# A new SBUF layout for the weight squares and the moved rows of an attention and MLP-mixer kernel

## The chip, the cores and the metric

The kernel runs on one core of a Trainium2 chip. The metric is device time in microseconds (us) of one execution. Engines are named as in the profile: PE is TensorE (PEld its weight loads), DVE VectorE, ACT ScalarE, POOL GpSimd, and SP the engine whose queue issues the loads. SBUF is the on-chip memory that the engines read from, PSUM the accumulators that TensorE writes.

## What is computed

Linear attention over 8 batches, 8 heads, 576 positions and 64 dimensions a head; its result goes through a token mixer and a channel mixer. All inputs are float32 (the weights arrive as 64-bit floats and are made narrower on the chip). Cut to what matters:

```
q_s = softmax(q, over dims);  k_s = softmax(k, over positions)
x   = q_s @ (k_s.T @ v)                          # [8, 576, 512]
u   = x + (relu(x.T @ w_tok1) @ w_tok2).T        # token mixer, 576 -> 256 -> 576
out = u + relu(u @ w_ch1) @ w_ch2                # channel mixer, 512 -> 1536 -> 512
```

## The kernel before

Products that need float32's precision are made of three: each factor is split into a high part (rounded to the type fp32r) and a low part (the rest), and high x high, low x high and high x low are summed in PSUM. `split` (L105, L106) does this: ScalarE copies the high part, VectorE subtracts it from the source and writes the low part.

**Units.** A unit is one batch and one pair of heads; there are 32. Each runs softmax of k and q, then four stages on TensorE: s1 (turning q, and k x v, L268), s2 (L328, the first token product), s3 (L336, and the first half of L373), s4 (the second half of L373). The first 8 units (two batches) are done in plain float32 while the weights arrive; the other 24, the late ones, are put between the steps described next by a table of places (`put`). A late unit's q is turned by VectorE and ScalarE (L306, L314) and split into `qth` and `qtl`. Stage L373 leaves `u`, turned and split, in the tiles `uh` and `ul`: four rows of 512 columns a group of 512 positions, three pairs of such tiles in turn.

**Steps.** The channel mixer runs over 9 groups of 512 positions and, for each, over 12 slices `f` of 128 hidden channels: 108 steps. A step is `ch1` and, one step behind, `ch2`.

- `ch1` (L402) makes 12 matmuls into one bank of PSUM: for each of four `n`, `c1h` x `uh`, `c1l` x `uh`, `c1h` x `ul`. What is held in TensorE is a square of weights (128 x 128, 512 bytes in each partition); what is moved through it is a row of `uh` or `ul` (512 columns, 2 KiB in each partition). ScalarE (L405) and VectorE (L406) then write relu of the result, split, to `h2h` and `h2l` (2 KiB each).
- `ch2` (L415) makes 12 matmuls into four banks, three for each `n`: `c2h` x `h2h`, `c2l` x `h2h`, `c2h` x `h2l`.

While a matmul moves its row, the next matmul's square is loaded; in the trace each weight load begins within 0.01 us of the start of the matmul ahead of it. So at each time TensorE reads two places of SBUF: the row of this matmul and the square of the next one.

**Weights.** `load_ch(f)` loads, narrows and splits the two slices of a step: 512 columns each of `w_ch1` and `w_ch2`. Slices 0 to 3 are loaded while the last early units run, 4 to 11 ahead of steps 1, 2, 4, 5, 7, 8, 10 and 11. Steps 0 to 3 are group 0, slices 0 to 3; then group 1 runs all slices, then group 0 the other eight, then the groups 2 to 8.

**Order and places.** The order of each engine's instructions is chosen when the program is built, by a scheduler that keeps the dependencies. The pools decide the addresses. In the built program the places in a partition are, modulo 2 KiB: squares n of `c1h` and `c1l` at 1536 + 512n; squares n of `c2h` and `c2l` at 1920 + 512n; the rows of `uh`, `ul`, `h2h`, `h2l` all at 1920. By **distance** the prediction means the start of the moved row less the start of the square loaded meanwhile, modulo 2 KiB. While square n of `ch1` is loaded it is 1920 - 1536 - 512n, so 384, 1920, 1408 and 896 for n = 0 to 3; in `ch2` it is -512n, so 0, 1536, 1024 and 512. Where a `ch1` matmul loads a square of `ch2` it is 0, and where a `ch2` matmul loads a square of `ch1` 384.

Of the kernel before, what the change touches and what calls it, by code (L numbers as in the profile page):

```python
# [8 lines left out]
F32 = mybir.dt.float32  # L9
F32R = mybir.dt.float32r  # L10
# [5 lines left out]
P = 128  # L16
CW = 512
# [3 lines left out]
def attn_mixer_kernel(ctx: ExitStack, tc: tile.TileContext, q, k, kt, v, wt, out, dims):  # L21
# [3 lines left out]
    nc = tc.nc  # L25
    B, H, S, D, TOK, DM, DCH, wide = dims
    NJ = DM // P
    NF = DCH // P
# [8 lines left out]
    F_HEAD, F_MORE = 4, 8  # L37

    const = ctx.enter_context(tc.tile_pool(name="const", bufs=1))
# [3 lines left out]
    sm = ctx.enter_context(tc.tile_pool(name="sm", bufs=2))  # L43
    stg = ctx.enter_context(tc.tile_pool(name="stg", bufs=2))
    cv = ctx.enter_context(tc.tile_pool(name="cv", bufs=2))
    upool = ctx.enter_context(tc.tile_pool(name="upool", bufs=1))
    hpool = ctx.enter_context(tc.tile_pool(name="hpool", bufs=2))
    ps_o = ctx.enter_context(tc.tile_pool(name="ps_o", bufs=NJ, space=bass.MemoryType.PSUM))
    ps_h = ctx.enter_context(tc.tile_pool(name="ps_h", bufs=4, space=bass.MemoryType.PSUM))

# [19 lines left out]
    def kv_tile(pool, i):  # L70

        t = pool.tile([P, P], F32, name=f"kvf{i}")
        nc.gpsimd.memset(t, 0.0)
        return t

    kv_ring = [kv_tile(const, 0)]

    w1h = const.tile([P, C, TOK], F32R, name="w1h")
    w1l = const.tile([P, C, TOK], F32R, name="w1l")
    w1th = const.tile([P, TOK], F32R, name="w1th")  # L80
    w1tl = const.tile([P, TOK], F32R, name="w1tl")
    w2h = const.tile([P, NT, S], F32R, name="w2h")
    w2l = const.tile([P, NT, S], F32R, name="w2l")
    c1h = const.tile([P, NF, NJ, P], F32R, name="c1h")
    c1l = const.tile([P, NF, NJ, P], F32R, name="c1l")
    c2 = {}

    def c2_rows(f0, f1):
        late = ctx.enter_context(tc.tile_pool(name=f"late{f0}", bufs=1))
        h_ = late.tile([P, f1 - f0, DM], F32R, name=f"c2h{f0}")  # L90
        l_ = late.tile([P, f1 - f0, DM], F32R, name=f"c2l{f0}")
        for f in range(f0, f1):
            c2[f] = h_[:, f - f0, :], l_[:, f - f0, :]

    c2_rows(0, F_HEAD)
    part = const.tile([P, NJ, CW], F32, name="part")

    Q = 32

    def f32(ap):  # L100
        return ap.bitcast(F32)

    def split(hi, lo, src, lo_eng):

        nc.scalar.copy(hi, src)  # L105
        lo_eng.tensor_tensor(lo, src, f32(hi), op=ALU.subtract)  # L106
# [3 lines left out]
    def ps_unit(dtype=F32):  # L110

        pools = unit_banks[0]
        pool, name = pools[turn[0] % len(pools)]
        turn[0] += 1
        return pool.tile([P, 512], dtype, name=name)
# [33 lines left out]
    def load_weights(i, n=CW, out=None):  # L149

        if not wide:
            t = out if out is not None else cv.tile([P, C1 * P], F32, name="cv_s")[:, 0:n]
            nc.sync.dma_start(t, wt[i][:, 0:n])
            return t
        conv.append(conv.pop(0))
        raw = conv[-1][0].tile([P, CW, 2], U32, name="stg")
        nc.sync.dma_start(raw[:, 0:n, :].rearrange("p n w -> p (n w)"), wt[i][:, 0:n].bitcast(U32))
        return narrow(raw, n, out)

    def narrow(raw, n, out):  # L160


        w0, w1 = raw[:, 0:n, 0], raw[:, 0:n, 1]
        s = conv[-1][1].tile([P, C1 * P], U32, name="cv_s")[:, 0:n]
        nc.vector.tensor_scalar(s, w1, 20, 0x7FF, op0=ALU.logical_shift_right, op1=ALU.bitwise_and)
        nc.scalar.activation(s, s, AF.Relu, bias=ebias, scale=2.0**23)
        nc.vector.scalar_tensor_tensor(s, w1, 0x80000000, s, op0=ALU.bitwise_and, op1=ALU.bitwise_or)
        nc.vector.tensor_scalar(w1, w1, 0xFFFFF, 0x100000, op0=ALU.bitwise_and, op1=ALU.bitwise_or)
        f1 = w1.bitcast(F32)
        nc.vector.scalar_tensor_tensor(f1, w0, 2.0**-32, w1, op0=ALU.mult, op1=ALU.add)  # L170
        z = s.bitcast(F32) if out is None else out
        nc.vector.tensor_tensor(z, f1, s.bitcast(F32), op=ALU.mult)
        return z
# [3 lines left out]
    AT_T1, AT_T2, AT_TAIL, AT_C1 = 0, N1, N1 + NT, N1 + NT + 2  # L177
    AT_C2 = AT_C1 + NF
# [18 lines left out]
        split(w2h[:, :, S0:S], w2l[:, :, S0:S], t, nc.vector)  # L197

    def load_ch(f):
        h_, l_ = (w[:, f].rearrange("p n m -> p (n m)") for w in (c1h, c1l))  # L200
        split(h_, l_, load_weights(AT_C1 + f), nc.vector)
        split(*c2[f], load_weights(AT_C2 + f), nc.vector)


    def softmax_k(u):
        ktt = u["kt"]
        mc = sm.tile([P, 1], F32, name="mc")
        nc.vector.tensor_reduce(mc, ktt, axis=AX.X, op=ALU.max)
        kx = u["k"]
        if u["early"]:  # L210
            nc.vector.tensor_scalar(mc, mc, -1.0, None, op0=ALU.mult)
            nc.scalar.activation(ktt, ktt, AF.Exp, bias=mc)
            t = ps_unit()
            for c in range(C):
                nc.tensor.transpose(t[:, c * P : (c + 1) * P], ktt[:, c * P : (c + 1) * P], f32(ident))
            nc.scalar.copy(kx[:, 0:C, :], t.rearrange("p (c d) -> p c d", c=C))
            t = ps_unit()
            nc.tensor.transpose(t[:, 0:P], ktt[:, S0 : S0 + P], f32(ident))
            nc.scalar.copy(kx[:, C, :], t[:, 0:P])
            return  # L220

        dg = sm.tile([P, P], F32, name="dg", bufs=1)
        nc.scalar.activation(dg, f32(ident), AF.Copy, scale=mc)
        t = ps_unit()
        nc.tensor.matmul(t[:, 0:P], ones, dg, start=True, stop=True)  # L225
        mb = sm.tile([P, P], F32, name="mb", bufs=1)
        nc.scalar.copy(mb, t[:, 0:P])  # L227
        nc.gpsimd.tensor_tensor(kx, kx, mb.unsqueeze(1).broadcast_to([P, C1, P]), op=ALU.subtract)  # L228
        nc.scalar.activation(kx, kx, AF.Exp)
# [115 lines left out]
        u["hh"], u["hl"] = hh, hl  # L345


    slots = [tuple(upool.tile([P, NJ, CW], F32R, name=f"u{x}{i}") for x in "hl") for i in range(3)]
    uT = [slots[i] for i in (0, 1, 2, 1, 0, 2, 1, 0, 2)]
    assert len(uT) == NG  # L350

# [40 lines left out]
            yield  # L392

    def ch1(g, f):
        hh = hpool.tile([P, CW], F32R, name="h2h")
        hl = hpool.tile([P, CW], F32R, name="h2l")
        t = ps_h.tile([P, 512], F32, name="ps_h")
        i = 0
        for n in range(NJ):
            uh, ul = (x[:, n, :] for x in uT[g])  # L400
            for a, w in ((c1h, uh), (c1l, uh), (c1h, ul)):
                nc.tensor.matmul(t, a[:, f, n, :], w, start=(i == 0), stop=(i == 3 * NJ - 1))  # L402
                i += 1
        drained[:] = [
            nc.scalar.activation(hh, t, AF.Relu).ins,  # L405
            nc.vector.scalar_tensor_tensor(hl, t, 0.0, f32(hh), op0=ALU.max, op1=ALU.subtract).ins,  # L406
        ]
        return hh, hl

    def ch2(acc, f, first, last, hh, hl):  # L410

        for n, o in enumerate(acc):
            cs = slice(n * P, (n + 1) * P)
            for i, (a, w) in enumerate(((c2[f][0], hh), (c2[f][1], hh), (c2[f][0], hl))):
                nc.tensor.matmul(o, a[:, cs], w, start=(first and i == 0), stop=(last and i == 2))  # L415

    def stage_rows():

# [97 lines left out]
                split_tok1()  # L516
    early_pools.close()
    del v_ring[1:], kv_ring[1:]
    ld = ctx.enter_context(tc.tile_pool(name="ld", bufs=2))
    wk = ctx.enter_context(tc.tile_pool(name="wk", bufs=1))  # L520
    c2_rows(F_HEAD, F_MORE)
    more_pools = ExitStack()
    stg_more = more_pools.enter_context(tc.tile_pool(name="stg_more", bufs=2))
    cv_more = more_pools.enter_context(tc.tile_pool(name="cv_more", bufs=2))
# [4 lines left out]
    steps = [(0, f) for f in range(F_HEAD)] + [(1, f) for f in range(NF)] + [(0, f) for f in range(F_HEAD, NF)]  # L529
# [14 lines left out]
    for n in range(NE, NU):  # L544
        b, j = divmod(n, NJ)
        if b == 2:
            at = (n0 - 10, n0 - 9, n0 - 9, n0 - 7.5) if j == 0 else [n0 - 9.5 + 2 * j + x for x in (0, 0.5, 1, 1.5)]
        else:
            at = [n0 + (b - 3) * NF + 3 * j + x for x in (0, 1, 1.5, 2)]
# [10 lines left out]
    for i, (g, f) in enumerate(steps):  # L560
        if i in load_at:
            if load_at[i] == F_MORE:
                more_pools.close()
                conv[:] = [(stg, cv)]
                c2_rows(F_MORE, NF)
            with behind(drained):
                load_ch(load_at[i])
        h = ch1(g, f)
        for fn in todo.pop(i, []):
            fn()  # L570
        if pend is not None:
            ch2(*pend[1:])
            if pend[0] != g:
                out_end(*pend[:2], i != F_HEAD)
        for fn in todo.pop(i + 0.5, []):
            fn()
        last = i + 1 == len(steps) or steps[i + 1][0] != g
        if pend is None or pend[0] != g:
            acc = [ps_o.tile([P, CW], F32, name="ps_o") for _ in range(NJ)]
        pend = (g, acc, f, pend is None or pend[0] != g, last, *h)  # L580
        if last and g > 1:
            residual(g)
# [60 lines left out]
```

## Time and profile before

| | us |
|---|---|
| executions | 834.90, 835.94, 837.50 |
| their median | 835.94 |
| the profiled execution: its span, first instruction to last | 835.7 |
| TensorE busy in the span | 805.4 |
| VectorE busy | 490.0 |
| ScalarE busy | 330.6 |

The page has one time for the profiled execution, its span. The slices of the page cut the span into 40 equal parts of 20.9 us; a digit is the busy share in tenths. The first two slices are the start (loads, first softmax); up to some 200 us the weights are converted on VectorE while the early units and the first steps run; behind that the steps and the late units alternate; the last 140 us are steps alone.

### The profile page before, as it was taken

The page shows a single profiled execution, that of the slowest core. Times are in us where ns is not written, and L with a number is a line of the kernel's source. Part 1 is how long each engine was busy: PE and PEld are TensorE (multiplying, and loading weights), DVE is VectorE, ACT ScalarE, POOL GpSimd, SP SyncE. Part 2 cuts the span into 40 slices and gives each one's busy share as a digit, 9 for nine tenths or more (in the row PEclk, how much of TensorE's full clock was granted, in tenths as well). Part 3 has the DMA queues.
Part 4 walks back from the last instruction along what each step waited for, and adds up shares of the span by engine and source line. Part 5 has one row for each costly group of instructions (what it writes and reads, how often), then busy time and mean ns, then how long its engine had stood idle before and what let it go on. Part 6 is the DMA issues. An engine that isn't in the chain of part 4 may idle for free.

```text
span 835.7 us, 11793 instructions
## 1 busy us (share of the span) xinstructions
PE 805.4 (96%) x4464; PEld 671.2 (80%) x4464; DVE 490.0 (59%) x1084; ACT 330.6 (40%) x822; POOL 113.2 (14%) x93
## 2 busy tenths in 40 slices
PE   3799999989999999999999999999999999999997
PEld 2588888777888888788888888888888888888885
DVE  6899998999775555655556554755565323012112
ACT  6876443554543344334434343444434421101110
POOL 1000000113220111311112111311131102001000
PEclk9999999999999999999999999999999999999999
DMA  8653523424212122322232211322131001001001
GB/s 269 204 144 111 201 103 99 130 62 137 85 41 94 56 62 54 105 62 62 62 112 62 62 51 33 106 61 61 32 96 46 15 1 51 1 0 51 1 1 50
DMA packets 60632, 63.54 MB, mean 76 GB/s; under 512 B 40864, under 2 KB 40992, under 8 KB 60576
## 3 DMA queue, kind: packets, MB, share of 16 engines
q1 hardware_dynamic: 55392, 53.36, 21.8%
q10 hardware_dynamic: 5184, 9.44, 3.0%
q8 instruction: 35, 0.57, 0.3%
q14 instruction: 21, 0.17, 0.1%
HBM read 53.35 MB, written 9.44 MB: 75 GB/s over the span
## 4 chain that ended last, share of the span: by engine, by line
PE 81%; DVE 8%; DMA 5%; ACT 3%; issue 2%; POOL 1%; SPq 1%; DVEq 0%; POOLq 0%; ACTq 0%
PE ps_h L402 32%; PE ps_o L415 31%; PE ps_h L373 6%; PE ps_h L328 5%; DVE q_t L314 2%; DMA q_t<-in_q 2%; PE ps_h L268 2%; DMA out<-stg 2%; PE ps_h L336 1%; ACT q_t L242 1%; PE ps_o L373 1%; PE ps_h L225 1%; DMA kt_t<-in_kt 1%; DVE st L236 1%; DVE qtl L106 1%
## 5 line engine op out<-in xcount | busy, mean ns | idle before, releaser
L406 DVE SCALAR_TENSOR_TENSOR h2l<-ps_h,h2h 128x512 fp32r<-128x512 f32 x108 | 74.3, 688 | 176.5 <-ACT h2h L405 176.5
L402 PE MATMUL ps_h<-uh,c1h 128*128 128x512 f32 x432 | 171.8, 398 | 0.0
L402 PE MATMUL ps_h<-ul,c1h 128*128 128x512 f32 x432 | 171.4, 397 | 0.0
L402 PE MATMUL ps_h<-uh,c1l 128*128 128x512 f32 x432 | 171.3, 396 | 0.0
L415 PE MATMUL ps_o<-h2h,c2h 128*128 128x512 f32 x432 | 169.2, 394 | 1.0 <-ACT h2h L405 1.0
L405 ACT ACTIVATE h2h<-ps_h 128x512 fp32r<-128x512 f32 x108 | 64.4, 597 | 266.0 <-PE ps_h L402 255.4
L415 PE MATMUL ps_o<-h2h,c2l 128*128 128x512 f32 x432 | 168.5, 391 | 0.0
L415 PE MATMUL ps_o<-h2l,c2h 128*128 128x512 f32 x432 | 152.1, 396 | 0.0
L314 DVE COPY q_t<-cv_s 32x160 f32<-32x160 f32 (+1 forms) x264 | 70.4, 267 | 61.7 <-POOL ql L106 58.4
L402 PEld LDWEIGHTS ps_h<-ul,c1h 128*128 128x128 f32 x432 | 81.8, 189 | 19.4
L415 PEld LDWEIGHTS ps_o<-h2h,c2h 128*128 128x128 f32 x432 | 81.2, 188 | 18.4 <-ACT h2h L405 1.4
L402 PEld LDWEIGHTS ps_h<-uh,c1l 128*128 128x128 f32 x432 | 81.9, 189 | 16.9
L402 PEld LDWEIGHTS ps_h<-uh,c1h 128*128 128x128 f32 x432 | 81.6, 189 | 17.1
L415 PEld LDWEIGHTS ps_o<-h2h,c2l 128*128 128x128 f32 x432 | 81.2, 188 | 16.8
L415 PEld LDWEIGHTS ps_o<-h2l,c2h 128*128 128x128 f32 x432 | 79.6, 188 | 16.4
L228 POOL TENSOR_TENSOR k_t<-k_t,mb 128x640 f32<-128x640 f32 x24 | 38.3, 1595 | 318.6 <-ACT mb L227 304.8
L106 POOL TENSOR_TENSOR ql<-q_t,qh 128x640 fp32r<-128x640 f32 x24 | 37.6, 1568 | 196.9 <-ACT qh L105 164.3
L428 POOL TENSOR_TENSOR stg<-uh,ul 128x512 f32<-128x512 f32 x28 | 35.5, 1289 | 144.6 <-DMA out<-stg 81.5
L236 DVE TENSOR_REDUCE st<-q_t 128x10 f32<-128x640 f32 x32 | 26.2, 818 | 40.3 <-DMA q_t<-in_q 40.3
L314 ACT COPY q_t<-cv_s 32x128 f32<-32x128 f32 (+1 forms) x120 | 36.8, 307 | 2.3 <-DVE cv_s L306 0.9
L247 ACT ACTIVATE q_t<-q_t 128x640 f32<-128x640 f32 x28 | 20.7, 740 | 42.9 <-DVE q_t L246 42.9
L373 PE MATMUL ps_h<-w2l,hh 128*128 128x256 f32 (+1 forms) x112 | 32.7, 296 | 0.1
(146 smaller groups left out, 1163.0 us busy)
## 6 DMA issues: line engine op xcount, KB each, us to landing
stg<-in_w SPq DMA_DIRECT2D x28, 512.0 KB, 3.4
kt_t<-in_kt SPq DMA_DIRECT2D x32, 320.0 KB, 3.4
q_t<-in_q SPq DMA_DIRECT2D x32, 320.0 KB, 2.9
v_t<-in_v SPq DMA_DIRECT2D x64, 128.0 KB, 3.0
out<-stg ACTq DMA_DIRECT2D x32, 256.0 KB, 2.8
k_t<-in_k SPq DMA_DIRECT2D x24, 320.0 KB, 3.6
v_t<-in_v SPq DMA_DIRECT2D x32, 32.0 KB, 3.1
out<-part ACTq DMA_DIRECT2D x4, 256.0 KB, 2.9
```

The lines of the kernel that those rows point to most:

```text
L106: lo_eng.tensor_tensor(lo, src, f32(hi), op=ALU.subtract)
L228: nc.gpsimd.tensor_tensor(kx, kx, mb.unsqueeze(1).broadcast_to([P, C1, P]), op=ALU.subtract)
L236: nc.vector.tensor_reduce(st[:, 0, :], qt, axis=AX.X, op=ALU.max)
L247: nc.scalar.activation(qc, qc, AF.Exp)
L314: eng(qx[ys, 0:n, xs], turned[xs, 0:n, ys])
L328: nc.tensor.matmul(y[:, 0:TOK], a, w, start=(i == 0), stop=(i == len(mm) - 1))
L373: nc.tensor.matmul(t[:, 0:N], a, w, start=(i == 0), stop=(i == len(mm) - 1))
L402: nc.tensor.matmul(t, a[:, f, n, :], w, start=(i == 0), stop=(i == 3 * NJ - 1))
L405: nc.scalar.activation(hh, t, AF.Relu).ins,
L406: nc.vector.scalar_tensor_tensor(hl, t, 0.0, f32(hh), op0=ALU.max, op1=ALU.subtract).ins,
L415: nc.tensor.matmul(o, a[:, cs], w, start=(first and i == 0), stop=(last and i == 2))
L428: nc.gpsimd.tensor_tensor(res[n], f32(uh), f32(ul), op=ALU.add)
```

## The change

The change lays the same data elsewhere and swaps the order of two matmuls. The number of instructions on each engine stays what it was (4002 matmuls and branches, 1086 rows on VectorE, 820 on ScalarE, 216 on SP, 98 on GpSimd).

1. The four squares of a step and an n stand side by side in one tile, 2 KiB: `c1h`, `c1l`, `c2h`, `c2l` at 0, 512, 1024, 1536 behind its start (`ch_rows`, index x = 0 to 3). Both slices of the weights go with the pools `late0`, `late4` and `late8`; before, `c1h` and `c1l` had places of their own for all slices.
2. `uh`, `ul`, `h2h` and `h2l` come from one pool with small tiles between them (`dg`, `mb`, `kvf0`) that shift the starts. `h2` is a pair of tiles in turn.
3. The low square comes first: in `ch1` `c1l` x `uh`, `c1h` x `uh`, `c1h` x `ul`; in `ch2` likewise.
4. The pool of the slices 4 to 7 is opened ahead of the pools of the late units, not behind them.

```diff
+    slots = [[None, None] for _ in range(3)]
+    for i in range(3):
+        slots[i][0] = lay.tile([P, NJ, CW], F32R, name=f"uh{i}")
+    dg = lay.tile([P, P], F32, name="dg")
+    for i in range(3):
+        slots[i][1] = lay.tile([P, NJ, CW], F32R, name=f"ul{i}")
+    mb = lay.tile([P, P], F32, name="mb")
+    h2 = [[lay.tile([P, CW], F32R, name=f"h2h{i}"), None] for i in range(2)]
+    kv_ring = [kv_tile(lay, 0)]
+    for i in range(2):
+        h2[i][1] = lay.tile([P, CW], F32R, name=f"h2l{i}")
...
-        h_ = late.tile([P, f1 - f0, DM], F32R, name=f"c2h{f0}")
-        l_ = late.tile([P, f1 - f0, DM], F32R, name=f"c2l{f0}")
+        t = late.tile([P, f1 - f0, NJ, 4, P], F32R, name=f"cw{f0}")
         for f in range(f0, f1):
-            c2[f] = h_[:, f - f0, :], l_[:, f - f0, :]
+            cw[f] = [t[:, f - f0, :, x, :] for x in range(4)]
...
     def load_ch(f):
-        h_, l_ = (w[:, f].rearrange("p n m -> p (n m)") for w in (c1h, c1l))
-        split(h_, l_, load_weights(AT_C1 + f), nc.vector)
-        split(*c2[f], load_weights(AT_C2 + f), nc.vector)
+        for x, at in ((0, AT_C1), (2, AT_C2)):
+            t = load_weights(at + f).rearrange("p (n m) -> p n m", n=NJ)
+            split(cw[f][x], cw[f][x + 1], t, nc.vector)
...
-            for a, w in ((c1h, uh), (c1l, uh), (c1h, ul)):
-                nc.tensor.matmul(t, a[:, f, n, :], w, start=(i == 0), stop=(i == 3 * NJ - 1))
+            for x, w in ((1, uh), (0, uh), (0, ul)):
+                nc.tensor.matmul(t, cw[f][x][:, n, :], w, start=(i == 0), stop=(i == 3 * NJ - 1))
...
-            for i, (a, w) in enumerate(((c2[f][0], hh), (c2[f][1], hh), (c2[f][0], hl))):
-                nc.tensor.matmul(o, a[:, cs], w, start=(first and i == 0), stop=(last and i == 2))
+            for i, (x, w) in enumerate(((3, hh), (2, hh), (2, hl))):
+                nc.tensor.matmul(o, cw[f][x][:, n, :], w, start=(first and i == 0), stop=(last and i == 2))
...
+    ch_rows(F_HEAD, F_MORE)
     ld = ctx.enter_context(tc.tile_pool(name="ld", bufs=2))
     wk = ctx.enter_context(tc.tile_pool(name="wk", bufs=1))
-    c2_rows(F_HEAD, F_MORE)
```

In the built program the places are now, modulo 2 KiB: squares `c1h`, `c1l`, `c2h`, `c2l` of every n at 1920, 384, 896 and 1408; rows of `uh` at 384, of `ul` at 896, of `h2h` at 1408, of `h2l` at 1920. So the distance is 512 for every n while a matmul of `ch1` loads the next square of `ch1`, and while one of `ch2` loads the next of `ch2`; it is 1536 where the one passes into the other. `w1h`, `w1l`, `w2h` and `w2l` stand 512 bytes lower than before, and the late units' tiles where they stood.

What the scheduler made of it shows in two places. First TensorE's order at the end of the last `ch1` of the program and the start of the `ch2` behind it, before (names with `_` and a number are tiles):

```order
L402 MATMUL ps_h<-uh_116,c1l 128x512
L402 MATMUL ps_h<-ul_117,c1h 128x512
L402 MATMUL ps_h<-uh_116,c1h 128x512
L402 MATMUL ps_h<-uh_116,c1l 128x512
L402 MATMUL ps_h<-ul_117,c1h 128x512
L415 MATMUL ps_o<-h2h,c2h_1377 128x512
L415 MATMUL ps_o<-h2h,c2l_1378 128x512
L415 MATMUL ps_o<-h2l,c2h_1377 128x512
```

and with the change, where one tile `cw` holds all four squares (so the two matmuls on `uh`, low square then high, read alike and stand as one row x2):

```order
L407 MATMUL ps_h<-uh_102,cw_1362 128x512 x2
L407 MATMUL ps_h<-ul_106,cw_1362 128x512
L407 MATMUL ps_h<-uh_102,cw_1362 128x512 x2
L407 MATMUL ps_h<-ul_106,cw_1362 128x512
L419 MATMUL ps_o<-h2h_108,cw_1362 128x512 x2
L419 MATMUL ps_o<-h2l_112,cw_1362 128x512
```

The sequence of rows moved (`uh`, `uh`, `ul`; `h2h`, `h2h`, `h2l`) is the same; only the squares ahead of it have changed places. Behind some 220 us of the profile before, every engine's order is the same as before but for this.

The second place is the first late unit. Before, TensorE reaches its first use of `qth` so:

```order
L328 MATMUL ps_h<-w1tl,qh 128x256
L415 MATMUL ps_o<-h2l,c2h_1377 128x512 x4
L402 MATMUL ps_h<-uh_114,c1l 128x512
L402 MATMUL ps_h<-ul_115,c1h 128x512
...
L336 MATMUL ps_h<-kvf_96,ys 128x128 x2
L373 MATMUL ps_h<-qth,kvh 128x320
L402 MATMUL ps_h<-uh_112,c1h 128x512
```

and with the change so (L335 was L328, L343 was L336, L379 was L373, L407 was L402):

```order
L335 MATMUL ps_h<-w1th,qh 128x256
L335 MATMUL ps_h<-w1tl,qh 128x256
L343 MATMUL ps_h<-kvf_110,ys 128x128 x2
L379 MATMUL ps_h<-qth,kvh 128x320
L407 MATMUL ps_h<-uh_100,cw_1067 128x512 x2
```

The four `ch2` and eleven `ch1` matmuls that stood between the unit's stages s2 and s3 now stand ahead of s2; the number of matmuls ahead of `qth` is 729 in both. VectorE there, before (c2l is the last split of weights):

```order
L306 STREAM_TRANSPOSE cv_s<-q_t 128x640
L106 TENSOR_TENSOR c2l_1378<-cv_s,c2h_1377 128x512
L106 TENSOR_TENSOR qtl<-q_t,qth 128x576
L314 COPY q_t<-cv_s 32x5x32 x6
L406 SCALAR_TENSOR_TENSOR h2l<-ps_h,h2h 128x512
```

and with the change:

```order
L313 STREAM_TRANSPOSE cv_s<-q_t 128x640
L115 TENSOR_TENSOR qtl<-q_t,qth 128x576
L115 TENSOR_TENSOR cw_1362<-cv_s,cw_1362 128x4x128
L351 SCALAR_TENSOR_TENSOR hl<-ps_h,hh 128x256
L321 COPY q_t<-cv_s 32x5x32 x6
```

The unit's low half `qtl` has passed the last split.

More of the change, by code (lines that the diff above doesn't have):

```diff
@@ L45, in attn_mixer_kernel @@
     cv = ctx.enter_context(tc.tile_pool(name="cv", bufs=2))
-    upool = ctx.enter_context(tc.tile_pool(name="upool", bufs=1))
-    hpool = ctx.enter_context(tc.tile_pool(name="hpool", bufs=2))
+    lay = ctx.enter_context(tc.tile_pool(name="lay", bufs=1))
     ps_o = ctx.enter_context(tc.tile_pool(name="ps_o", bufs=NJ, space=bass.MemoryType.PSUM))
@@ L74, in kv_tile @@
         return t
-    kv_ring = [kv_tile(const, 0)]
     w1h = const.tile([P, C, TOK], F32R, name="w1h")
@@ L83, in attn_mixer_kernel, with ch_rows @@
     w2l = const.tile([P, NT, S], F32R, name="w2l")
[L84 to L88, printed above, removed]
+    part = const.tile([P, NJ, CW], F32, name="part")
+    slots = [[None, None] for _ in range(3)]
[9 more added lines that the diff above has]
+        h2[i][1] = lay.tile([P, CW], F32R, name=f"h2l{i}")
+    cw = {}
+    def ch_rows(f0, f1):
         late = ctx.enter_context(tc.tile_pool(name=f"late{f0}", bufs=1))
-        h_ = late.tile([P, f1 - f0, DM], F32R, name=f"c2h{f0}")
-        l_ = late.tile([P, f1 - f0, DM], F32R, name=f"c2l{f0}")
+        t = late.tile([P, f1 - f0, NJ, 4, P], F32R, name=f"cw{f0}")
         for f in range(f0, f1):
-            c2[f] = h_[:, f - f0, :], l_[:, f - f0, :]
-    c2_rows(0, F_HEAD)
-    part = const.tile([P, NJ, CW], F32, name="part")
+            cw[f] = [t[:, f - f0, :, x, :] for x in range(4)]
+    ch_rows(0, F_HEAD)
     Q = 32
@@ L220, in softmax_k @@
             return
-        dg = sm.tile([P, P], F32, name="dg", bufs=1)
         nc.scalar.activation(dg, f32(ident), AF.Copy, scale=mc)
@@ L225, in softmax_k @@
         nc.tensor.matmul(t[:, 0:P], ones, dg, start=True, stop=True)
-        mb = sm.tile([P, P], F32, name="mb", bufs=1)
         nc.scalar.copy(mb, t[:, 0:P])
@@ L345, in stage_h1 @@
         u["hh"], u["hl"] = hh, hl
-    slots = [tuple(upool.tile([P, NJ, CW], F32R, name=f"u{x}{i}") for x in "hl") for i in range(3)]
     uT = [slots[i] for i in (0, 1, 2, 1, 0, 2, 1, 0, 2)]
@@ L394, in ch1 @@
     def ch1(g, f):
-        hh = hpool.tile([P, CW], F32R, name="h2h")
-        hl = hpool.tile([P, CW], F32R, name="h2l")
+        hh, hl = h2[steps.index((g, f)) % 2]
         t = ps_h.tile([P, 512], F32, name="ps_h")
@@ L412, in ch2 @@
         for n, o in enumerate(acc):
-            cs = slice(n * P, (n + 1) * P)
-            for i, (a, w) in enumerate(((c2[f][0], hh), (c2[f][1], hh), (c2[f][0], hl))):
-                nc.tensor.matmul(o, a[:, cs], w, start=(first and i == 0), stop=(last and i == 2))
+            for i, (x, w) in enumerate(((3, hh), (2, hh), (2, hl))):
+                nc.tensor.matmul(o, cw[f][x][:, n, :], w, start=(first and i == 0), stop=(last and i == 2))
     def stage_rows():
@@ L564, in attn_mixer_kernel @@
                 conv[:] = [(stg, cv)]
-                c2_rows(F_MORE, NF)
+                ch_rows(F_MORE, NF)
             with behind(drained):
```

## The prediction

> **What bounds the kernel now.** I read the page's engine table first, then the slices, then the chain that ended last, and last the groups of instructions.
>
> ```profile
> PE 805.4 (96%) x4464; PEld 671.2 (80%) x4464; DVE 490.0 (59%) x1084; ACT 330.6 (40%) x822; POOL 113.2 (14%) x93
> PE   3799999989999999999999999999999999999997
> DVE  6899998999775555655556554755565323012112
> PEclk9999999999999999999999999999999999999999
> PE 81%; DVE 8%; DMA 5%; ACT 3%; issue 2%; POOL 1%; SPq 1%; DVEq 0%; POOLq 0%; ACTq 0%
> L402 PE MATMUL ps_h<-uh,c1h 128*128 128x512 f32 x432 | 171.8, 398 | 0.0
> L415 PE MATMUL ps_o<-h2h,c2l 128*128 128x512 f32 x432 | 168.5, 391 | 0.0
> ```
>
> TensorE is busy 96% of the span at the full granted clock, makes 81% of the chain, and the groups of L402 and L415, six of 432 matmuls each (2592 in all), wait for nobody. A duration (398 ns) overlaps the next matmul, so it says nothing of the pace. The pace is in the chain in order of time, where consecutive matmuls of one line stand as one piece (start, length, what):
>
> ```profile
> 109.88 7.44 PE ps_h L402 x32
> 117.33 5.45 PE ps_o L415 x24
> ...
> 254.39 5.47 PE ps_o L415 x24
> ...
> 761.29 2.80 PE ps_h L402 x12
> 764.09 2.76 PE ps_o L415 x12
> ...
> 775.15 2.73 PE ps_o L415 x12
> 777.88 2.80 PE ps_h L402 x12
> 780.68 2.76 PE ps_o L415 x12
> ```
>
> This is what I argue from. Shape, type and clock are the same in every piece, nobody waits, yet L402 runs at 2.80/12 = 233.3 ns a matmul (7.44/32 = 232.5) and L415 at 2.76/12 = 230.0, at 2.73/12 = 227.5 in one step, and at 5.45/24 = 227.1 and 5.47/24 = 227.9 where 24 of them follow each other. Near the end, where almost only TensorE works, 2.80 and 2.76 alternate, so it is no disturbance by other engines. Something in the two lines' operands costs L402 some 6 ns each time, and L415 some 3 ns after a change from the other line, and it dies out as the run of L415 gets longer. One matmul at a time (timeline, TensorE's rows; start, length):
>
> ```profile
> 752.81 0.40 PE L415 MATMUL ps_o<-h2h,c2h 128*128 128x512 f32 x1
> 753.05 0.39 PE L415 MATMUL ps_o<-h2h,c2l 128*128 128x512 f32 x1
> 753.27 0.39 PE L415 MATMUL ps_o<-h2l,c2h 128*128 128x512 f32 x1
> ...
> 754.66 0.39 PE L415 MATMUL ps_o<-h2l,c2h 128*128 128x512 f32 x1
> 754.89 0.39 PE L415 MATMUL ps_o<-h2h,c2h 128*128 128x512 f32 x1
> 755.11 0.39 PE L415 MATMUL ps_o<-h2h,c2l 128*128 128x512 f32 x1
> 755.34 0.40 PE L415 MATMUL ps_o<-h2l,c2h 128*128 128x512 f32 x1
> 755.57 0.40 PE L402 MATMUL ps_h<-uh,c1h 128*128 128x512 f32 x1
> 755.81 0.40 PE L402 MATMUL ps_h<-uh,c1l 128*128 128x512 f32 x1
> ```
>
> From start to start the group begins with 0.24 and 0.22, ends with 0.23, 0.22 and 0.23 (754.66 to 755.34: 0.68/3 = 227), and the first of L402 takes 0.24. What differs between the lines is the place of the moved row against the square loaded meanwhile: in L415 the distance is always a multiple of 512 bytes (0, 1536, 1024, 512 modulo 2 KiB as n goes from 0 to 3), in L402 at the last of its twelve alone (else 384, 1920, 1408, 896: 384 modulo 512). So I read: at multiples of 512 the pace settles at 227 ns within some eight matmuls, whichever multiple it is; at 384 modulo 512 it never settles and averages 233.
>
> **The change part by part.** *The layout, L402.* All distances of L402 become 512 modulo 2 KiB, at the step's last matmul 1536: multiples of 512. By the reading above its matmuls go from 232.5 to 233.3 down to 227.1, and 1296 x 5.4 to 6.2 ns = 7.0 to 8.1 us are gone. I take 7.6.
>
> *The layout, L415.* It is no longer thrown off by L402 before it. Its groups stand at 230.0 where L402 comes first and at 227.9 where 24 run on; the gain is 1296 x 0.8 to 2.9 = 1.0 to 3.8 us. I take 2.4, the middle, since both kinds recur all along. Both lines together: 10.0 us.
>
> *What is not realized.* Until about 212 us VectorE sets the pace, and a faster TensorE only waits longer:
>
> ```profile
> 160.00:212.00 52.00, 48.21 (x287) 40.02 (x286) 47.50 (x101) 26.18 (x64) 10.95 (x7) 0.97 0.34 105
> 0.00:200.00 200.00, 58.12 (x226) 43.43 (x227) 0.99 0.48 149
> 200.00:836.00 636.00, 266.38 (x1072) 198.78 (x1070) 1.00 0.18 53
> PE ps_h L373 <- ACT qth L105: 2.6, 1, 2.6
> ```
>
> The first row is the table by stretches (length, then busy us of TensorE, weight loads, VectorE, ScalarE, GpSimd): VectorE works 47.5 of 52 us, converting the last weights and turning the first late head pair. The next two are the same table for L402 alone: 226 of 1298 records, 17%, lie before 200 us. I take 17% of 10.0 = 1.7 us as lost to waits like the one in the last row: 8.3 left. The bound is that all of it is kept.
>
> *Settling after the other stages.* The table by stretches for TensorE's work on ys alone (four records of L336 a head pair) gives
>
> ```profile
> 212.00:836.00 624.00, 13.31 (x88) 1.00 0.18 52
> ```
>
> so 22 head pairs stand between the steps behind 212 us, each with four bursts of other matmuls (L268, L328, L336 with L373, L373), whose operands the change leaves where they are modulo 512 bytes: w1h, w1l, w2h and w2l move down by exactly 512. If the pace has to settle after each burst, that costs what the group 2.76 has over 2.73, 0.03 us: 22 x 4 x 0.03 = 2.6 us at most and nothing at best. I take 0.7, since part of it is in today's groups too and already counted as staying: the 5.47 at 254 us begins behind a burst. 7.6 left.
>
> *Low square first.* It only permutes two of three matmuls that are there before. The one on the low square now opens the group, so a step waits for VectorE's part of the split where it waited for ScalarE's. Four steps' squares are split while the early pairs run and the others some steps ahead of their use; the page has no wait of L402 for a split, and I cost it at nothing. If a step caught it, the price is one such subtraction, once:
>
> ```profile
> L106 DVE TENSOR_TENSOR c1l<-cv_s,c1h 128x512 fp32r<-128x512 f32 x12 | 8.3, 690 | 0.1
> L106 DVE TENSOR_TENSOR w2l<-cv_s,w2h 128x128 fp32r<-128x128 f32 x1 | 0.3, 288 | 0.0
> L381 DVE TENSOR_TENSOR ul<-ps_h,uh 128x128 fp32r<-128x128 f32 x12 | 3.4, 287 | 0.0
> ```
>
> *Split writes in four pieces.* Each of the 48 writes into the squares goes to four runs of 128 elements, 2 KiB apart. The nearest rows: 128 columns written as two runs (w2l) take 288 ns, as one run (ul) 287. I take nothing; 1 ns for each run more would be 48 x 3 = 0.1 us, against or for.
>
> *Pools.* The first eight squares' sets and the late pairs' buffers now lie over other early buffers. The order shows what came of it up to 212 us: the same 729 matmuls stand ahead of the first late pair's first use of qth, but the eleven L402 that stood between L328 and that use now stand ahead of L328, and VectorE's qtl comes ahead of the last square's split instead of behind it. What this does to the wait of 2.6 us is bounded by the row of the wait and by the slow matmuls behind it:
>
> ```profile
> 176.68 0.63 PE L402 MATMUL ps_h<-uh,c1l 128*128 128x512 f32 x1
> 177.11 0.63 PE L402 MATMUL ps_h<-ul,c1h 128*128 128x512 f32 x1
> ...
> 179.24 0.63 PE L402 MATMUL ps_h<-uh,c1l 128*128 128x512 f32 x1
> 179.67 0.44 PE L402 MATMUL ps_h<-ul,c1h 128*128 128x512 f32 x1
> ```
>
> Behind the wait seven matmuls start (179.67 - 176.68)/7 = 0.43 us apart instead of 0.23 (granted clock 0.97 in the stretch above), 7 x 0.2 = 1.4 us. So the place may give 2.6 + 1.4 = 4.0 us or cost as much again. VectorE's work there is the same, so I take 0 and put half of it, 2 us, into the range.
>
> Sum: 835.7 (span) - 7.6 = 828.1. The median of the runs shown, 835.94, is 0.2 above the span, so the forecast is **828.3**. Its own range: 824.5 with everything kept and no settling (11.9 us is the most both lines give), to 832.
>
> **Two pages against the trace.** The rows above have the same shape and clock at 233.3 and at 227.1 ns. The Trainium skill, page "SBUF — State Buffer", section "Who interferes with whom", says that TensorE's two read ports, for the moved operand and for the weight load, are independent, and that "PE and ACT never wait on anyone." By that rule the placement of rows and squares changes nothing and the time stays at 835.9. The trace speaks against it as far as equal matmuls at unequal pace can; no run here yet moves an operand alone. The Trainium skill, page "TensorE: Matmul & The Clock Gate", section "Wait — 56ns, not 53.3ns?", gives 215.7 ns for 512 columns; by that every matmul here has some 11 ns to lose even at its best, an estimate of another 2592 x 11.4 = 30 us that no piece of this trace shows.
>
> **The rivals.** *No change.* The 6 ns are not of the distance but of L402's own pattern, twelve matmuls into one bank of PSUM against L415's three into each of four; then neither line moves, since L415 is thrown off by L402 as before. For it: both patterns change at the same place as the distance, so the trace cannot part them. Against it: L415's pace dies down to 227 whichever bank it is on. 835.9, with the pools' 2 us either way 834 to 837.
>
> *Slower: 512 is the wrong multiple.* If a steady 512 holds the cycle that L402 shows, L415 loses the pace it has: from 230.0 or 227.9 up to 233.3, 1296 x 3.3 to 5.4 = 4.3 to 7.0 us: 840 to 843. It decides on whether L415's 12-groups last longer than 2.76. Against it: at n = 3 L415 has just this distance, and there the starts are 0.22 to 0.23 apart.
>
> *Much faster: 512 is better than the other multiples.* The trace has starts 0.22 apart after 0.24 (753.05 to 753.27). If every matmul went at 220 to 224, the gain beside what I count is 2592 x 3 to 7 = 8 to 18 us: 810 to 820. Against it: L415's starts at n = 3 are no nearer to each other than at the other multiples once settled.
>
> **How the numbers follow.** Forecast 0.72; no change 0.13; slower 0.08; much faster 0.07. The forecast's own range, 824.5 to 832, leaves out the last two and the no-change case; to leave out no more than 2 in 10 the range has to reach into no change, so it goes up to 836.5, and down to 822.5 for the pools' place. A measurement of this kernel can tell about 0.3%, 2.5 us, from no change. Faster by more: 0.72 + 0.07 less the forecast's upper tail = 0.78. Within: 0.14. Slower by more: 0.08.
>
> **What would show it.** Right: in the chain behind 220 us the pieces of L402 and L415 both last 2.72 to 2.74 for 12, also where they alternate near the end, and TensorE's wait near 170 us is some 1 to 2 us longer. The first step is wrong if L402 stays at 2.80; the second, if L415 stays at 2.76 with L402 at 2.73; the third, if the first late pair's qth is reached earlier by the same 1.7 us; the settling, if pieces behind a burst last 0.03 longer than others. The whole is wrong if pieces go above 2.80, or below 2.70.

## The result and the profile after

The changed kernel takes **829.91 us** (median of 4 runs, 828.82 to 830.65) beside 835.98 us for the kernel before on the same chip (4 runs, 834.9 to 837.5): a ratio of 0.9921, 95% interval 0.9906 to 0.9936. In a later series it took 828.24 us (827.0 to 828.74) beside 835.84: 0.9908 (0.9895 to 0.9922). The forecast was 828.3, faster.

First the page of the changed kernel: its span, the engine table, the chain that ended last by engine, and the first two groups of instructions. L407 is the old L402 (`ch1`), L419 the old L415 (`ch2`).

```profile
span 828.3 us, 11791 instructions
PE 796.6 (96%) x4464; PEld 669.5 (81%) x4464; DVE 487.7 (59%) x1084; ACT 331.6 (40%) x822; POOL 113.0 (14%) x93
PE 77%; DVE 11%; DMA 6%; issue 2%; ACT 2%; POOL 1%; SPq 1%; DVEq 0%; POOLq 0%; ACTq 0%
L407 PE MATMUL ps_h<-uh,cw 128*128 128x512 f32 x864 | 268.3, 391 | 1.3 <-DVE cw L115 1.3
L419 PE MATMUL ps_o<-h2h,cw 128*128 128x512 f32 x864 | 250.0, 391 | 0.0
```

The span went from 835.7 to 828.3, and TensorE's busy time from 805.4 to 796.6, with the same 4464 matmuls; no other engine's work moved by more than 2.3 us. Two things stand here that the text ahead did not have. The profiled execution of the changed kernel took 830.2 us by the clock outside, 1.9 more than its span. With that much around it the profiled execution before took 837.5, the highest of its runs, and not a time near their median. And L407 has one wait of 1.3 us for a split of weights.

The chain in order of time (start, length, what), among the late units and then near the end:

```profile
205.78 2.72 PE ps_h L407 x12
208.50 1.68 PE ps_h L335 x14
210.18 2.77 PE ps_o L419 x12
...
222.43 2.72 PE ps_h L407 x12
225.15 1.68 PE ps_h L335 x14
226.82 2.77 PE ps_o L419 x12
...
749.72 2.72 PE ps_h L407 x12
752.44 2.72 PE ps_o L419 x12
755.16 2.72 PE ps_h L407 x12
757.88 2.72 PE ps_o L419 x12
```

Where the lines alternate, 2.80 and 2.76 have become 2.72 and 2.72: 226.7 ns a matmul in both. Behind a burst of other matmuls (L335) the piece lasts 2.77, 0.05 longer.

TensorE's waits between 150 and 212 us (us in total, times, longest):

```profile
PE ps_h L343 <- ACT ys L337: 2.2, 1, 2.2
PE ps_h L379 <- DVE hl L351: 1.4, 1, 1.4
PE ps_h L407 <- DVE cw L115: 1.3, 1, 1.3
PE ps_o L419 <- DVE h2l L411: 1.0, 1, 1.0
```

Before, the same stretch had these:

```profile
PE ps_h L373 <- ACT qth L105: 2.6, 1, 2.6
PE ps_o L415 <- ACT h2h L405: 0.7, 1, 0.7
PE ps_h L373 <- DVE hl L344: 0.5, 1, 0.5
```

The wait of 2.6 us of the first `qth` is gone, and four others stand in its place; together the waits there grew from 3.8 to 5.9 us.

One difference between the two profiles is not of the change. By the table by stretches (length, then busy us of TensorE, weight loads, VectorE, ScalarE, GpSimd, then the granted clock, the DMA share and GB/s) TensorE's clock was lower for a while in the execution before (first row) and not in the one after (second row):

```profile
160.00:185.00 25.00, 22.44 (x121) 18.32 (x120) 23.37 (x52) 13.62 (x32) 3.15 (x2) 0.93 0.26 73
160.00:185.00 25.00, 21.50 (x143) 17.76 (x142) 23.97 (x54) 13.71 (x33) 4.81 (x3) 1.00 0.32 92
```

The seven slow matmuls that the prediction shows there, 1.4 us, lie in this stretch of lower clock. The prediction took them for something that the pools' place might give. Of the twelve profiled executions of the whole kernel in this document seven have 0.93 in this stretch and five 1.00, in the old places and in the new ones alike.

**Where the 7.4 us came from.** From 205 us on, TensorE's order is the same in both kernels but for the two squares, so its records can be summed by kind of matmul, from the start of one to the start of the next. The cut is the 877th matmul of the program. The prediction's column is its own sum, 83% of the two lines' gain behind the cut:

| us | before | after | difference | predicted |
|---|---|---|---|---|
| start of the 877th matmul | 204.9 | 203.3 | -1.6 | 0 |
| `ch1`, 1068 matmuls | 250.1 | 244.9 | -5.2 | -6.3 |
| `ch2`, 1077 matmuls | 251.0 | 249.7 | -1.3 | -2.0 |
| settling behind other stages | in the two rows above | in the two rows above | | +0.7 |
| the units' own matmuls, some 1250 records | 120.4 | 121.2 | +0.8 | 0 |
| waits and the end | 9.3 | 9.2 | -0.1 | 0 |
| span | 835.7 | 828.3 | -7.4 | -7.6 |

The sum is right to 0.2 us in these two executions because its steps missed in opposite directions: late gains were too high, an early one was left out. That they cancel so well is luck, and the first row holds the stretch of lower clock too. The runs below take the steps one by one.

### The profile page after: what moved, and what is told of

It is laid out like the page before. It is cut to its first block, busy times and chain, and to the rows that moved or that the text cites. A ratio compares the mean times of both kernels' runs of the same rounds, so it can differ in the third digit from the quotient of the medians.

```text
span 828.3 us, 11791 instructions
## 1 busy us (share of the span) xinstructions
PE 796.6 (96%) x4464; PEld 669.5 (81%) x4464; DVE 487.7 (59%) x1084; ACT 331.6 (40%) x822; POOL 113.0 (14%) x93
## 4 chain that ended last, share of the span: by engine, by line
PE 77%; DVE 11%; DMA 6%; issue 2%; ACT 2%; POOL 1%; SPq 1%; DVEq 0%; POOLq 0%; ACTq 0%
PE ps_h L407 30%; PE ps_o L419 30%; PE ps_h L379 6%; PE ps_h L335 5%; DVE q_t L321 3%; DMA out<-stg 2%; PE ps_h L275 2%; DMA q_t<-in_q 2%; PE ps_h L343 1%; PE ps_o L379 1%; DMA stg<-in_w 1%; PE ps_h L233 1%; DVE st L243 1%; POOL ql L115 1%; DMA kt_t<-in_kt 1%
## 5 line engine op out<-in xcount | busy, mean ns | idle before, releaser
L407 PE MATMUL ps_h<-uh,cw 128*128 128x512 f32 x864 | 268.3, 391 | 1.3 <-DVE cw L115 1.3
L419 PE MATMUL ps_o<-h2h,cw 128*128 128x512 f32 x864 | 250.0, 391 | 0.0
L419 PEld LDWEIGHTS ps_o<-h2h,cw 128*128 128x128 f32 x864 | 160.2, 188 | 32.6 <-ACT h2h L410 0.2
L407 PEld LDWEIGHTS ps_h<-uh,cw 128*128 128x128 f32 x864 | 159.3, 188 | 32.4 <-DVE cw L115 1.7
L407 PE MATMUL ps_h<-ul,cw 128*128 128x512 f32 x432 | 168.6, 390 | 0.0
L410 ACT ACTIVATE h2h<-ps_h 128x512 fp32r<-128x512 f32 x108 | 64.6, 598 | 251.0 <-PE ps_h L407 234.6
L419 PE MATMUL ps_o<-h2l,cw 128*128 128x512 f32 x432 | 151.9, 395 | 1.0 <-DVE h2l L411 1.0
L407 PEld LDWEIGHTS ps_h<-ul,cw 128*128 128x128 f32 x432 | 81.1, 188 | 17.4
L419 PEld LDWEIGHTS ps_o<-h2l,cw 128*128 128x128 f32 x432 | 79.6, 188 | 17.4 <-DVE h2l L411 1.4
L379 PE MATMUL ps_h<-w2h,hl 128*128 128x320 f32 (+1 forms) x112 | 30.1, 302 | 4.3 <-DVE hl L351 4.1
L379 PE MATMUL ps_h<-w2h,hh 128*128 128x256 f32 (+1 forms) x112 | 32.7, 299 | 0.0
L379 PE MATMUL ps_h<-w2l,hh 128*128 128x256 f32 (+1 forms) x112 | 32.6, 296 | 0.0
```

Of the source, the lines that this page charges most:

```text
L379: nc.tensor.matmul(t[:, 0:N], a, w, start=(i == 0), stop=(i == len(mm) - 1))
L407: nc.tensor.matmul(t, cw[f][x][:, n, :], w, start=(i == 0), stop=(i == 3 * NJ - 1))
L419: nc.tensor.matmul(o, cw[f][x][:, n, :], w, start=(first and i == 0), stop=(last and i == 2))
```

## The experiments

Two theories were put to test. One is the prediction's: the pace hangs on the **distance** between the start of the moved row and the start of the square loaded meanwhile. The other is that it hangs on the pattern in PSUM, the order of the squares or the new order of the start.

**The order of the squares alone**, in the kernel before:

```diff
-            for a, w in ((c1h, uh), (c1l, uh), (c1h, ul)):
+            for a, w in ((c1l, uh), (c1h, uh), (c1h, ul)):
...
-            for i, (a, w) in enumerate(((c2[f][0], hh), (c2[f][1], hh), (c2[f][0], hl))):
+            for i, (a, w) in enumerate(((c2[f][1], hh), (c2[f][0], hh), (c2[f][0], hl))):
```

> The kernel before with the low square first in ch1 and ch2 and nothing else. Theory (the distance between the moved row and the square loaded meanwhile sets the pace, by its remainder modulo 512 bytes): c1h and c1l have the same remainders, so ch1 stays at 384 and ch2 at 0, the pieces of 12 stay at 2.80 and 2.76 us, and the time stays within 0.2% of before, 834.5 to 837.5 us. Rival (the order of the squares brought part of the 6 us): 830 to 833.

Measured: 835.76 us (834.65 to 836.64), ratio 1.000 (0.9987 to 1.0014). Its chain near the end still has the old pieces:

```profile
708.41 2.80 PE ps_h L402 x12
711.21 2.76 PE ps_o L415 x12
```

The order of the squares brings nothing.

**The high square first again**, in the changed kernel. The distances become 0, 512 and 1024:

```diff
-            for x, w in ((1, uh), (0, uh), (0, ul)):
+            for x, w in ((0, uh), (1, uh), (0, ul)):
...
-            for i, (x, w) in enumerate(((3, hh), (2, hh), (2, hl))):
+            for i, (x, w) in enumerate(((2, hh), (3, hh), (2, hl))):
```

> The changed kernel with the high square first again, so that the distances are 0, 512 and 1024 modulo 2 KiB, a third of the matmuls at each. Theory (any multiple of 512 does): pieces of 12 at 2.72 us, 828.5 to 831.5 us, as the changed kernel. Rival (512 modulo 2 KiB alone is good): two thirds of 2592 matmuls lose 3 to 6 ns each, pieces at 2.75 to 2.80, 835 to 840 us.

Measured: 827.45 us (825.19 to 828.56), ratio 0.9902 (0.9872 to 0.9933), and the pieces

```profile
708.36 2.72 PE ps_h L407 x12
711.08 2.72 PE ps_o L419 x12
```

So 512 is not singled out; 0 and 1024 do as well. (The changed kernel has these in places too, where matmuls of `h2l` stand next to each other: row at 1920, square `c2h` at 896.) A second series, beside the changed kernel on one chip, was to tell the two orders apart:

> The changed layout with the high square first once more. Theory (which of the two comes first is the same to the pace, and its 827.5 against 829.9 was the start's spread): 0.990 to 0.994 of before, as the changed kernel beside it, behind matmul 876 within 1 us of it. Rival (high first is better, since a step then does not wait for the low part of a split): 2 us faster than the changed kernel, its interval apart from it.

Measured: 828.41 (825.42 to 830.09), ratio 0.9911 (0.9893 to 0.9929), beside 828.24 for the changed kernel, whose own expectation was:

> The changed kernel once more, beside the next two on the same chip. Theory: 0.990 to 0.994 of before; behind the first 876 matmuls, where every engine's order is that of before, 619 to 620 us; the start varies by 2 us from run to run whatever the kernel. Rival (the change also made the start faster): matmul 876 starts 1.5 us or more ahead of before again.

The two orders cannot be told apart. For the start it was the rival that came: in this profile of the changed kernel the 877th matmul begins at 201.5 us, against 204.9 and 204.0 in two of the kernel before. From there to the start of the last matmul it takes 618.1 us, a little under the 619 to 620 expected, and with the high square first 617.5.

**Both lines put back at 384 modulo 512**, with nothing else of the change undone, by 128 bytes between the rows and the squares (two one-column tiles share a place to make room):

```diff
+    gap = lay.tile([P, 32], F32, name="gap")
+    nc.gpsimd.memset(gap, 0.0)
     cw = {}
```

> The changed kernel with a gap of 128 bytes ahead of the squares, so that every distance is 384 modulo 512 in ch1 and ch2. The products of w1 with the late units' q come to 0 modulo 512 by it (they were at 128). Theory: both lines at 2.80 for 12; 2592 x 6.2 ns = 16 us slower than the changed kernel, less the 2 to 3 us of settling that it has now: 842 to 845 us. Rival (the pace is the line's own, by its pattern in PSUM): ch1 at 2.80, ch2 at 2.73 to 2.76, 834 to 838. If nothing of the layout matters, 830.

Measured: 839.93 us (837.54 to 841.88), ratio 1.0047 (1.003 to 1.0064). The chain near the end:

```profile
707.85 2.79 PE ps_o L421 x12
710.64 2.79 PE ps_h L409 x12
713.44 2.78 PE ps_o L421 x12
```

This is the run that decides. Now `ch2` (L421) has the slow pace too, which it did not have before the change, while its pattern in PSUM is as it always was. The size falls 2 to 5 us short of what was expected, because the expectation set the settled 226.7 against 233 for every matmul. Behind the cut the means are 232.9 against 228.2 ns for `ch1` and 234.1 against 230.4 for `ch2`, as many groups of the changed kernel have not settled.

**Only `ch1` put back at 384**: the same gap between the rows of u and those of h.

```diff
     mb = lay.tile([P, P], F32, name="mb")
+    gap = lay.tile([P, 32], F32, name="gap")
+    nc.gpsimd.memset(gap, 0.0)
     h2 = [[lay.tile([P, CW], F32R, name=f"h2h{i}"), None] for i in range(2)]
```

> The changed kernel with the gap of 128 bytes between the rows of u and those of h: ch1 at 384 modulo 512, ch2 at 0, as before the change, in the new layout. Theory: the old pieces come back, 2.80 for ch1 and 2.76 for ch2 where ch1 is ahead of it; behind 212 us the time is that of before, the start that of the changed kernel: 833.5 to 837 us. Rival (the gain was that the squares stand side by side, or another order of the start): 829 to 831.

Measured: 834.65 us (833.39 to 838.15), ratio 0.9991 (0.9972 to 1.0011), and the old pieces of `ch1` are back:

```profile
709.37 2.79 PE ps_h L409 x12
712.16 2.73 PE ps_o L421 x12
714.90 2.79 PE ps_h L409 x12
```

For `ch2` (L421) the expectation missed: 2.73 behind such a `ch1`, and not the 2.76 of before. Behind the 877th matmul `ch1` takes 249.9 us here, as before the change (250.1), but `ch2` takes 249.8, as in the changed kernel (249.7). So the gain of `ch1`, 5.2 of the 6.5 us that the two lines won there, hangs on where the rows of u stand against its squares; that of `ch2` did not need it.

**The distance by itself.** A probe: 48 matmuls in a row on one square for each distance, each row of 48 behind five of 256 columns that throw the pace off.

```diff
+    for d in DS:
+        e = block(f"d{d}", [(0, 2048 + d // 4, 512)] * K)
+    for d in (512, 384):
+        e = block(f"far{d}", [(0, 4096 + d // 4, 512)] * K)
+        e = block(f"two{d}", [(0, 1024 + d // 4, 512), (0, 3072 + d // 4, 512)] * (K // 2))
+        e = block(f"mv{d}", [(64, 2048 + 64 + d // 4, 512)] * K)
```

> A probe: it leaves the whole computation out and runs 48 matmuls in a row at each of 29 distances between the moved row (512 columns) and the square loaded meanwhile, each row behind five matmuls of 256 columns at a distance of 128; then the distances 512 and 384 with a row 8 KiB away, with two rows in turn, and with row and square both 256 bytes further; ahead of them 256 and 320 columns at 0, 128, 256 and 384. Theory (the remainder modulo 512 decides): 0, 512, 1024 and 1536 settle at 227 ns (48 in 10.9 us), 384 and 896, 1408, 1920 stay at 233 (48 in 11.2 us), the same with a far row, with two rows and with both moved. Rival (512 modulo 2 KiB alone): only 512 at 227. Rival (neither): one pace for all. Open: where between 384 and 512 the pace changes, and whether 256 and 320 columns go faster at 0 than at 128.

Its chain in order of time. The distances of these pieces are 0, 16, 64, 128, 256, 384, 496, 512, 640 and 768 bytes, then 512 with a farther row and 384 with a farther row:

```profile
64.76 10.89 PE t L39 x48
76.25 11.12 PE t L39 x48
...
99.77 11.00 PE t L39 x48
...
123.14 11.14 PE t L39 x48
...
146.68 10.88 PE t L39 x48
...
169.74 11.20 PE t L39 x48
...
205.10 11.33 PE t L39 x48
...
217.03 10.91 PE t L39 x48
...
263.63 11.20 PE t L39 x48
...
275.42 10.89 PE t L39 x48
...
403.61 10.88 PE t L39 x48
...
438.14 11.20 PE t L39 x48
```

With nothing but the address changed, 48 matmuls take 10.88 to 10.91 us at one set of distances and 11.00 to 11.33 at the others. The mean of the last thirty, from start to start:

```
226.7 ns   0 256 512 768 1024 1280 1536 1792
228.9      64 320 576
231.6      16 528
232.2      128
233.3      32 96 192 384 448 480 544 640 896 1152 1408 1664 1920 1984
236.7      496
```

The step is **256 bytes**, not 512. The prediction's good distances (0, 512, 1024, 1536) are half of the set; its bad ones (384, 896, 1408, 1920) are all 128 modulo 256. A farther row, two rows in turn, and row and square moved together gave the same as the plain distance. No distance went below 226.7.

The probe leaves one rival. Its square stands at one place in all pieces but two, and in those two row and square moved by 256 bytes, which is the step itself. So by the probe alone the place of the row modulo 256 could count, without the square. The kernels decide this. Before the change the rows of both lines stood at the same place (1920), and `ch2` was fast and `ch1` slow. With `ch1` alone put back, the squares of both lines stood multiples of 512 bytes apart in one tile, and again `ch2` was fast and `ch1` slow. Neither the place of the row nor that of the square sets the pace by itself. The runs show what the pace depends on, not the part of the chip that causes it.

**The units' rows at a multiple too.** In the units' products w1 and w2 are the rows that are moved. In the changed kernel they go up by 384 bytes, so that the products with w1 stand at 0 modulo 512:

```diff
+    sm = ctx.enter_context(tc.tile_pool(name="sm", bufs=2))
     const = ctx.enter_context(tc.tile_pool(name="const", bufs=1))
...
-    sm = ctx.enter_context(tc.tile_pool(name="sm", bufs=2))
```

> The changed kernel with the pool of small tiles ahead of the others, so that w1 and w2 stand 384 bytes higher: the products of w1 with the late units' q go from a distance of 128 modulo 512 to 0. Everything of ch1 and ch2 stays. Theory: those products do not go faster (the probe has 120 ns for 256 columns at 0, 119 at 128), but ch2 settles sooner behind them (28 ns lost for each of 22 units in the run with the gap, 53 in the changed kernel): 0.5 us faster than the changed kernel, too little to tell in time. Rival (the units' products gain as ch1 did, 3%): 22 x 14 x 3.5 ns = 1.1 us, and 2 us with the settling.

Measured: 828.25 us (827.02 to 828.76), ratio 0.9906 (0.989 to 0.9922), the same as the changed kernel. Its chain behind L335:

```profile
208.82 2.75 PE ps_o L419 x12
...
225.45 2.75 PE ps_o L419 x12
```

The burst ahead does set how long the pace takes to settle: 2.75 where the changed kernel has 2.77 (53 ns lost behind L335 there, 27 here). By 22 units that is 0.6 us, under what the series can tell.

**The start.** Three more runs, to see where the first 205 us got shorter:

> The kernel before once more, for the start of matmul 876 (204.9 us in its first profile, 203.1 with the low square first alone). Both theories: 203 to 205. It gives the spread of the start in the old order.

> The changed layout with every distance at 384 modulo 512, once more, for the start of matmul 876 (203.5 and 205.0 us in the two runs with the gap, 200.5 to 203.3 in the five with multiples of 512). Theory (the early steps' pace is realized too, since VectorE does not set the pace all along): again 203 to 205. Rival (the start gained by its new order of loads alone): 200.5 to 203, as the others of that order.

> The changed layout with the rows of u alone at 384 modulo 512, once more, for the start of matmul 876. Theory: 202 to 205, between the changed kernel and the one with both at 384. Rival: 200.5 to 203.

They took 837.49, 840.42 and 834.05 us, one execution each. The start of the 877th matmul in all profiled executions; an asterisk marks a granted clock of 0.93, not 1.00, between 160 and 185 us:

| | us | mean |
|---|---|---|
| order and pace of before (before, again) | 204.9\*, 204.0\* | 204.4 |
| low square first in the kernel before, pace of before | 203.1 | |
| new order of the start, both lines at 384 | 203.5\*, 205.0 | 204.3 |
| new order, `ch1` at 384 | 205.0\*, 203.1 | 204.1 |
| new order, multiples of 256 (changed twice, units' rows) | 203.3, 201.5\*, 202.0\* | 202.3 |
| high square first in the changed kernel, multiples of 256 | 200.8, 200.5\* | 200.6 |

The two rows with the squares swapped stand apart, since the scheduler gave each of them an order of the start of its own. In the rows of the new order the matmuls up to the 877th come in one and the same order, and there the pace brings some 1.9 us. The new order with the old pace is not ahead of the old order. Single executions of one kernel lie up to 2 us apart, and the stretch of lower clock does not sort them, so the sign is likely and the size is not settled.

## Why the prediction was right, and where its sum was not

*The distance is what counts*: right. It made both lines slow at 384 modulo 512 and one of them slow alone, in a program that is otherwise the changed one. "No change", by the pattern in PSUM, fell with the slow `ch2` of the gap. "Slower" fell with 2.72 at a steady 512. "Much faster" fell with the probe: no distance settles below 226.7.

*"At multiples of 512 the pace settles"*: true, but too narrow. Any multiple of 256 does. The trace of before held only distances that are multiples of 128, so it could not show this.

*"The layout, L402"*: 6.3 us expected behind the cut, 5.2 measured. The settled pace is as taken (2.72 for 12). The rest is settling, which the prediction had as a term of its own: `ch1` has a mean of 228.2 ns there, not 227.1, since pieces behind a burst begin with slow matmuls again.

*"The layout, L415"*: 2.0 expected, 1.3 measured. **This term was applied to matmuls that it does not concern.** It gave the gain of no longer being thrown off by L402 to all 1296. Of the matmuls of `ch2` behind the cut whose follower is of `ch2` too, only about a third (353 of 985) stand in a piece behind `ch1`. Their mean went from 229.4 to 226.7, which is 1.0 us. The other two thirds follow a unit's burst. The largest such kind, the pieces longer than 12 behind L335, stands at 229.0 where it stood at 228.6. The run with `ch1` alone at 384 shows a second fault: `ch2` has its gain there although the `ch1` ahead of it still throws it off. A piece of 12 behind `ch1` then loses 15 ns against the settled pace where it lost 36 before the change, and behind L337, the old L328, a piece loses 28 where the changed kernel loses 53.

*"Settling after the other stages"*: taken at 0.7 us, within a bound of 2.6. Counted against 226.7, the four bursts of a unit cost 53, 24, 28 and 25 ns in the changed kernel, 0.13 us for 22 units: 2.8 us. Part of it was there before, as the step said. The two lines came 1.8 us short of their gross gain (8.3 expected, 6.5 had), where the step allowed 0.7.

*"What is not realized"*: **this step failed.** It wrote off 1.7 us before 212 us because VectorE "sets the pace there". The sign it named for its own failure came: TensorE reaches the 730th matmul, at the first late pair's `qth`, at 174.2, 172.9 and 173.6 us in the changed places, and at 175.6, 175.2 and 174.3 in the old ones, 1.5 earlier on the mean (the first three are the changed kernel twice and the one with the units' rows moved, the others the kernel before twice and with the low square first). The new order with the gap, in which only the pace differs, has 175.5, 176.7, 175.5 and 174.1 there. At the 877th it is some 1.9. The waits did grow, as expected: from the 691st matmul to the 730th it took 11.3 us, and 10.2 before. But TensorE had come there 2.5 us earlier in these two executions, so the wait took back a part and not the whole. VectorE, busy 47.5 us of 52 there, could start some of its work earlier too; that is read from the times, and no run isolates it.

*"Low square first"* and *"split writes in four pieces"*: nothing in the time, as said, though a split was caught once (the 1.3 us of L407 above, about two such subtractions of 0.69). The order alone gave 1.000, and the reverse order in the changed kernel gave the same time as the changed kernel.

*"Pools"*: taken at 0 with 2 us of range. The new order without the new pace stands at 204.1 to 204.3 where the old one stands at 204.4: 0 within the spread, as taken. The wait of 2.6 us went, and its like came back under other names. The 1.4 us of slow matmuls that the range counted in were the stretch of lower clock, which comes and goes from one execution to the next in the old places and in the new.

*The base.* The sum set the span, 835.7, beside the median of the runs, 835.94, and called the median "0.2 above the span". A run takes 1.7 to 2.1 us more than its span here, 1.8 in the kernel before run again, so the execution in the profile was one of 837.5, 1.5 above the median. The forecast is not moved by this, since it is the median less a difference. But the differences of the table are between an execution 1.5 above its median and one 0.3 above its own: of the 7.4 us between the spans 1.3 are such scatter, and the medians fell by 6.1 in the first series and by 7.6 in the later one.

*Two small slips.* The two groups do not quite "wait for nobody": `ch2`'s matmuls waited 1.0 us in all for `h2h`, too little to bear on the sum. And 11.9 us below the median is 824.0, not 824.5.

*Left open.* The units' own matmuls take 120.8 to 121.5 us in every run with the new places, the two kernels with the gap included, and 120.4 to 120.6 with the old ones, long gaps left out. Putting the products with w1 at a multiple did not take this back (121.3).

*The two pages.* The Trainium skill, page "SBUF — State Buffer", section "Who interferes with whom", has TensorE's two read ports independent and says that "PE and ACT never wait on anyone." The probe differs: the same matmul beside the same load takes 226.7 to 236.7 ns by their distance alone, so for two operands of one engine the measurement decides; which part of the chip is the cause stays open. The Trainium skill, page "TensorE: Matmul & The Clock Gate", section "Wait — 56ns, not 53.3ns?", gives 215.7 ns for 512 columns; no settled pace here is below 226.7, with a square loaded beside each matmul.

## What to carry to other kernels

Where matmuls of one shape, none of them waiting, run at two paces in one trace, compare operand addresses before engines: here the start of the moved row against the start of the square loaded meanwhile, modulo 256 bytes. This is shown for fp32r matmuls of 512 columns alone. A gain per matmul holds only for those that stand behind the disturbance which goes, so count by what precedes a group and not by line. And a gain in a stage where another engine is busy 91% of the time is not lost there by that alone: bound it from both sides.

## What the runs showed that was not expected

The pace at a good distance is reached by way of a fixed sequence. Behind L335 the starts of the changed kernel follow each other by 240, 235, 229, 231, 231, 236, 228, 233, 231 ns and then by 227, 227, 226 for as long as the run of matmuls lasts; behind other bursts the same steps begin at another place. At a bad distance the steps between 228 and 241 recur without end (241, 232, 231, 232, 228, 230, 232 and again 241 for `ch1` before; 229 and 238 in turn for `ch1` put back). A distance of 64 modulo 256 lies between, at 228.9, and 496 is worse than all others, at 236.7.

In the probe, rows of 320 columns ran at 146.7 ns at 0, 128, 256 and 384 bytes alike: the distance cost nothing at that length.
